# Large loads issued by GpSimd instead of SyncE in a decode attention and feed-forward kernel

## The chip, the cores and the metric

The kernel runs on one core of a Trainium2 chip. A core has five engines that each work through a queue of their own: TensorE (PE, matrix products), VectorE (DVE), ScalarE (ACT), GpSimd (POOL) and SyncE (SP, which only issues transfers and waits). Sixteen DMA engines carry data between memory (HBM) and the core's on-chip buffer. The metric is device microseconds (us) from launch to end; the median of a few executions is given.

## The reference, cut to what matters

One decoding step for four sequences: attention over a cache of 4096 positions with 32 heads, a gated feed-forward block beside it, and a sigmoid gate that mixes the two. Everything is float32.

```
x: (4, 1, 512)   k_cache, v_cache: (4, 32, 4096, 128)
g = sigmoid((x * gate_w).sum(-1))
q = x @ wq                                   # 512 x 4096
p = softmax((q . k_cache) * 128 ** -0.5)     # per sequence and head
a = (p . v_cache) @ wo                       # wo 4096 x 512
b = (gelu(x @ w_gate) * (x @ w_up)) @ w_down # 512 x 1792, 512 x 1792, 1792 x 512
out = g * a + (1 - g) * b
```

The keys and values are 268 MB each, the weights together 28 MB. Each byte is read once.

## The kernel before, in words

The caches are cut into 32 blocks (`NT`), numbered `i`; block `i` holds four heads of one sequence. A block of keys or of values is one load of 128 partitions x 16384 float32, 64 KB for each partition, 8.389 MB in all. Everything large lives in one buffer, `big`, in which zones are handed on by offset: `wq` lies where the values will lie (`VA`), the gate weight `w_gate` follows `wq` in the same place, key blocks alternate between two zones that overlap by a quarter, and values have one zone.

For each block VectorE does the work on the keys in two parts, because the two key zones share a quarter: first the shared quarter (`products(i, True)`, line 384, then `sums(i, True)`, line 390), after which the next key block may land, then the other three quarters (`products(i, False)`, `sums(i, False)`), then three short steps of `soft_max`. ScalarE makes the weights `PM` (line 402). TensorE multiplies them with the values in `pv(i - 1)` (line 416), after which the next value block may land.

`Plan` records every step in program order with the bytes that it reads and writes, and works out for each what it has to wait for. Steps of PE, DVE and ACT are played in loops; steps of the other engines are written out one by one. A step's `lane` names the semaphore that it counts up: a load has one that belongs to its zone or tensor, whichever engine issues it.

All large loads go through one helper, `load` (line 258): `wq`, the key and value blocks, the feed-forward weights, and `wo` in eight pieces at the end. The rest are two small loads that ScalarE issues (`x` and `gate_w`) and two stores of the result that SyncE issues (line 616).

The opening, that is the load of `wq`, the two small loads and the load of key block 0, is played inside a critical section of the tile framework; then the framework's context is closed, and all that follows is played without it:

```
with tc.tile_critical(sync_engine=mybir.EngineType.Pool, no_gpsimd_drain=True):
    plan.play(plan.steps[:opening])
tc.close()
```

`tc.close()` puts a barrier of all five engines into the program, twice, in which GpSimd is the engine that gathers the others' arrivals and releases them. Each engine's part of it begins with a drain, an instruction that lets the engine's earlier work end first. Only behind it stand the steps that prepare `x` (GpSimd's identity matrix `ident`, TensorE's transposes at line 312, VectorE's copies `xT` at line 317), the projection of the queries (line 330), the folding of the query onto its heads (lines 347 to 374), and the loads of `w_gate` and `w_up`, which wait until TensorE has used `wq`.

Of the kernel before, what the change touches and what calls it, by code (L numbers as in the profile page):

```python
# [19 lines left out]
class Plan:  # L20
# [18 lines left out]
    def add(self, engine, emit, reads=(), writes=(), lane=None, unit=1):  # L39
        lane = lane or engine  # L40
        self.units[lane] = unit
        row = self.by_lane.setdefault(lane, [])
        step = Step(lane, engine, emit, self.turn if engine in self.loops else None)
        step.at = len(row)
        need = {}
        for accesses, writing in ((reads, False), (writes, True)):
            for name, lo, hi in accesses:
                for other, a, b, wrote in self.past.get(name, ()):
                    if a < hi and lo < b and (wrote or writing):
                        if other.lane == engine and engine == "pe":  # L50
                            continue
                        if other.lane == engine and not wrote:
                            continue
                        need[other.lane] = max(need.get(other.lane, -1), other.at)
        seen = self.seen[engine]
        for l, n in sorted(need.items(), key=lambda x: -len(self.by_lane[x[0]])):
            if seen.get(l, -1) >= n:
                continue
            other = self.by_lane[l][n]
            other.asked = True  # L60
            step.waits[l] = n
            seen[l] = n
            for k, v in self.knew[other].items():
                seen[k] = max(seen.get(k, -1), v)
        step.waits = {l: n for l, n in step.waits.items()
                      if not any(self.knew[self.by_lane[m][k]].get(l, -1) >= n for m, k in step.waits.items() if m != l)}
        self.knew[step] = dict(seen)
        self.knew[step][lane] = step.at
        if row and lane == engine:
            for k, v in self.knew[row[-1]].items():  # L70
                if k != lane:
                    self.knew[step][k] = max(self.knew[step].get(k, -1), v)
        for accesses, writing in ((reads, False), (writes, True)):
            for name, lo, hi in accesses:
                old = self.past.get(name, [])
                if writing:
                    old = [x for x in old if not (lo <= x[1] and x[2] <= hi)]
                self.past[name] = old + [(step, lo, hi, writing)]
        row.append(step)
        self.steps.append(step)  # L80
        return step
# [51 lines left out]
def tile_gated_mix(tc: tile.TileContext, x, kc, vc, wq, wo, w_gate, w_up, w_down, gate_w, out):  # L133
    nc = tc.nc
# [108 lines left out]
    add = plan.add  # L243
    V, A, T, G = nc.vector, nc.scalar, nc.tensor, nc.gpsimd
# [11 lines left out]
        return g if plan.k is None else plan.k  # L256

    def load(dst, src, writes, lane):
        return add("sp", lambda: nc.sync.dma_start(dst, src), (), writes, lane=lane, unit=16)

    def load_kv(kind, i):
        src = (vc, kc)[kind == "k"]
        a = KB_ * (i % 2) if kind == "k" else VA if i < NT - 1 else 0
        s = src[i % B, HT * (i // B):HT * (i // B) + HT].rearrange("h (p r) d -> (h p) (r d)", p=PH)
        load(place(a, TW), s, [z(a, TW)], "vl" if kind == "v" and i == NT - 1 else kind)
# [7 lines left out]
    def load_f(s):  # L273
        load(place((F0, F1)[s], KC * F), (w_gate, w_up)[s].rearrange("(p c) n -> p (c n)", c=KC),
             [z((F0, F1)[s], KC * F)], f"f{s}")

    def load_d():
        load(place(D0, FC * DM), w_down.rearrange("(p i) n -> p (i n)", i=FC), [z(D0, FC * DM)], "k")
# [326 lines left out]
    for h in range(2):  # L605
# [4 lines left out]
        for c, move in ((2 * h + 1, act), (2 * h, dve)):  # L610
            dst, read, write = res[:B, slice(*COLS[c])], [(("acc", "po0")[h], 0, C4)], [("res", *COLS[c])]
# [46 lines left out]
```

## Time and profile before

| | |
|---|---|
| median of 3 runs | 1309.09 us (1309.06 to 1309.27) |
| span of the profiled execution, first to last instruction | 1307.7 us |
| around it, to the median | 1.4 us |
| HBM read | 564.67 MB, 432 GB/s over the span |
| busy: PE, DVE, ACT, POOL | 354.1, 1158.2, 87.3, 0.7 us |

The time of the profiled execution itself is given as its span alone; what launch and end add is taken as the 1.4 us between it and the median. Busy times are sums over a span in which several engines work side by side. In the rows of the trace "SPq" is an instruction with which SyncE issues a transfer (it ends long before the transfer does), and "<-" behind a row names what ended the idle time ahead of it. "Landing" is the point at which all 16 DMA engines have reported the end of a transfer.

### The profile page before, as it was taken

How to read it: one execution, taken by the hardware profiler on the slowest of the kernel's cores; microseconds unless marked ns; L12 is line 12 of the kernel's file. 1: busy time of each engine (PE TensorE's matmuls, PEld its weight loads, DVE VectorE, ACT ScalarE, POOL GpSimd, SP SyncE). 2: the span in 40 equal slices, each digit the busy share in tenths (PEclk: the TensorE clock that was granted, in tenths of full speed). 3: DMA queues.
4: the chain of work that ended last, by engine and by line, in shares of the span. 5: the costliest groups of instructions: out<-in, count | busy, mean ns of one | idle time of the engine just before them, and what ended most of it. 6: DMA issues, size and time to landing. Idle time of an engine off the chain costs nothing.

```text
span 1307.7 us, 6169 instructions
## 1 busy us (share of the span) xinstructions
PE 354.1 (27%) x2512; PEld 100.8 (8%) x2512; DVE 1158.2 (89%) x303; ACT 87.3 (7%) x291; POOL 0.7 (0%) x6
## 2 busy tenths in 40 slices
PE   3402233201332211322221223321133322122227
PEld 0100001000010000100000000100001000000002
DVE  1899999999899998989989888998989898898992
ACT  0000000000000000000000000000000000000001
POOL 0000000000000000000000000000000000000000
PEclk9656666556666556666656666665666665576669
DMA  9999999999999999999999999999999999999998
GB/s 417 417 446 427 440 439 425 443 425 443 427 441 425 441 425 441 431 437 439 427 443 425 443 427 441 425 441 425 441 431 437 439 427 443 425 443 427 439 428 370
DMA packets 10986, 564.83 MB, mean 432 GB/s; under 512 B 1232, under 2 KB 1752, under 8 KB 1888
## 3 DMA queue, kind: packets, MB, share of 16 engines
q1 hardware_dynamic: 10960, 564.67, 99.7%
q8 instruction: 7, 0.11, 0.0%
q10 hardware_dynamic: 16, 0.02, 0.0%
q14 instruction: 3, 0.02, 0.0%
HBM read 564.67 MB, written 0.01 MB: 432 GB/s over the span
## 4 chain that ended last, share of the span: by engine, by line
DMA 71%; DVE 28%; issue 1%; PE 0%; ACT 0%; SPq 0%; DVEq 0%; POOLq 0%
DMA big<-in_A_k_cache 69%; DVE big L384 14%; DVE sc L390 13%; DMA big<-in_A_wo 2%; PE acc L505 0%; PE wide L497 0%; PE po L505 0%; DVE hT L537 0%; DVE big L535 0%; DVE big L534 0%; DVE big L532 0%; ACT big L511 0%; DVE m L395 0%; ACT big L533 0%; DVE big L530 0%
## 5 line engine op out<-in xcount | busy, mean ns | idle before, releaser
L384 DVE TENSOR_TENSOR big<-big,qb 128x4096 f32<-128x4096 f32 x64 | 556.0, 8687 | 88.8 <-DMA big<-in_A_k_cache 88.8
L390 DVE TENSOR_REDUCE sc<-big 128x32 f32<-128x4096 f32 x64 | 555.9, 8686 | 2.3
L416 PE MATMUL po<-big,PM 128*32 128x512 f32 x2048 | 293.4, 737 | 903.1 <-DMA big<-in_A_v_cache 903.1
L416 PEld LDWEIGHTS po<-big,PM 128*32 128x32 f32 x2048 | 72.3, 132 | 1117.8 <-DMA big<-in_A_v_cache 825.2
L402 ACT ACTIVATE PM<-sc,nb 32x128 f32<-32x128 f32 x128 | 67.2, 525 | 476.5 <-DVE nb L397 429.0
L424 ACT ACTIVATE o<-po 128x512 f32<-128x512 f32 x16 | 9.6, 597 | 443.9 <-PE po L416 443.9
L402 ACT ACTIVATION_READ_ACCUMULATOR PM<-sc,nb 32x1 f32 x128 | 26.1, 204 | 0.0
L374 ACT ACTIVATE qb<-q 128x512 f32<-128x512 f32 x8 | 4.8, 597 | 249.6 <-PE q L372 249.6
L347 DVE TENSOR_TENSOR big<-po,amask 128x512 f32<-128x512 f32 x2 | 1.3, 686 | 19.3 <-PE po L330 19.3
L433 PE MATMUL sm<-o,sel 128*16 128x128 f32 x128 | 15.4, 273 | 5.8 <-ACT o L424 5.8
L330 PE MATMUL po<-big,xT 128*32 128x512 f32 x64 | 10.0, 793 | 18.6 <-DMA big<-in_A_wq 18.6
L518 PE MATMUL q<-big,xT 128*32 128x448 f32 x64 | 10.8, 848 | 13.7 <-DMA big<-in_B_w_gate 11.0
L433 PEld LDWEIGHTS sm<-o,sel 128*16 128x16 f32 x128 | 11.7, 97 | 14.4 <-ACT o L424 13.1
L615 DVE COPY res<-acc 4x144 f32<-4x144 f32 x1 | 0.3, 296 | 13.2 <-PE acc L505 13.2
L372 PE MATMUL q<-QM,hc 128*128 128x512 f32 x16 | 9.9, 706 | 4.2 <-DVE hc L368 4.2
L395 DVE TENSOR_REDUCE m<-sc 128x1 f32<-128x128 f32 x32 | 9.2, 286 | 1.1
L440 DVE RECIPROCAL ri<-sm 16x1 f32<-16x1 f32 x8 | 1.2, 156 | 8.2 <-PE sm L435 8.2
L396 DVE STREAM_TRANSPOSE mt<-m 128x32 f32<-128x32 f32 x32 | 6.8, 212 | 1.1
L397 DVE TENSOR_REDUCE nb<-mt 128x1 f32<-128x32 f32 x32 | 6.0, 186 | 1.1
L497 PE MATMUL wide<-big 128*32 128x512 f32 x46 | 5.6, 596 | 2.3 <-DMA big<-in_A_wo 2.3
L518 PEld LDWEIGHTS q<-big,xT 128*32 128x32 f32 x64 | 3.3, 159 | 20.5 <-issue 20.5
L330 PEld LDWEIGHTS po<-big,xT 128*32 128x32 f32 x64 | 2.7, 139 | 25.1 <-issue 25.1
(74 smaller groups left out, 58.3 us busy)
## 6 DMA issues: line engine op xcount, KB each, us to landing
big<-in_A_wo SPq DMA_DIRECT2D x1, 4096.0 KB, 28.7
big<-in_B_w_gate SPq DMA_DIRECT2D x1, 3584.0 KB, 17.6
big<-in_B_w_up SPq DMA_DIRECT2D x1, 3584.0 KB, 25.8
big<-in_B_w_down SPq DMA_DIRECT2D x1, 3584.0 KB, 19.4
big<-in_A_wo SPq DMA_DIRECT2D x1, 1792.0 KB, 26.3
big<-in_A_wo SPq DMA_DIRECT2D x1, 1280.0 KB, 29.0
big<-in_A_k_cache SPq DMA_DIRECT2D x32, 29.7
big<-in_A_v_cache SPq DMA_DIRECT2D x32, 29.4
```

What stands on the lines that cost most here:

```text
L330: last = T.matmul(PO[s][32 * j:32 * j + 32].rearrange("p j d -> p (j d)"), xTf[:, c, :32], w[:, n0:n0 + HB * D], start=c == 0, stop=c == K ...
L372: pe(lambda: T.matmul(q.rearrange("p b d -> p (b d)"), HC.rearrange("p h k -> p (h k)"), QM.rearrange("p b d -> p (b d)"), start=True, sto ...
L384: dve(lambda: V.tensor_tensor(k, k, QB[:, b:b + 1, :].to_broadcast([P, r1 - r0, D]), op=OP.mult), m + t("qb"), m)
L390: dve(lambda: V.tensor_reduce(SC[i % 2][:, r0:r1], k, axis=AX.X, op=OP.add), [z(KA(i) + r0 * D, (r1 - r0) * D)], [(f"sc{i % 2}", r0, r1)])
L395: dve(lambda: V.tensor_reduce(M1[n], SC[n], axis=AX.X, op=OP.max), t(f"sc{n}"), t(f"m1{n}"))
L396: dve(lambda: V.transpose(MT, M1[n].to_broadcast([P, PH])), t(f"m1{n}"), t("mt"))
L397: dve(lambda: V.tensor_reduce(NB[n], MT, axis=AX.X, op=OP.max, negate=True), t("mt"), t(f"nb{n}"))
L402: last = A.activation(PM[:, PZ:].rearrange("p (c m) -> p c m", m=32)[s, :, h:RJ * HT:HT], SC[n][s, :].rearrange("p (c j) -> p c j", j=RJ), ...
L416: last = T.matmul(PO[n][32 * c:32 * c + 32].rearrange("p j d -> p (j d)"), PM[:, m0:m0 + 32], place(VAT(i) + j * N, N), start=b == 0 and j ...
L424: act(lambda: A.activation(O[n], PO[n], AF.Copy), t(f"po{n}"), t(f"o{n}"))
L433: T.matmul(sm[:B * HT, :D], selv[:, j, m0:m0 + B * HT], O[n][:, j, :], start=(n, j) == (0, 0), stop=(n, j) == (N - 1, RJ - 1))
L518: last = T.matmul(q.rearrange("p b d -> p (b d)")[32 * j:32 * j + 32, :FG], xTf[:, c, :32], place((F0, F1)[s] + c * F + j * FG, FG), start ...
```

## The change: who issues the loads

The helper `load` records its step for GpSimd instead of SyncE, and issues it there. Every load that goes through it moves; the waits worked out for it and the semaphore that it counts up stay. A transfer that SyncE issues uses a hardware queue, one that GpSimd issues a software queue.

```
     def load(dst, src, writes, lane):
-        return add("sp", lambda: nc.sync.dma_start(dst, src), (), writes, lane=lane, unit=16)
+        return add("pool", lambda: G.dma_start(dst, src), (), writes, lane=lane, unit=16)
```

The rows of the built program on GpSimd around the opening; "barrier ... gather" is the barrier of `tc.close()`, `Pool_sequencer_49`, `Pool_49` and `Activation_sequencer_49` belong to the critical section, L298 and L299 make `ident`. Drains are not listed among the rows: one stands on GpSimd directly ahead of each of the two barriers, before and now. Before:

```order
L622 NO_OP
L625 UNCONDITIONAL_BRANCH
L622 NO_OP [waits SP_sequencer_49,Activation_sequencer_49,Pool_sequencer_49]
L625 UNCONDITIONAL_BRANCH
L625 ISA [waits barrier_Pool_Activation_PE_DVE_SP_gather]
L298 MEMSET ident 128x128 [waits barrier_Pool_Activation_PE_DVE_SP_gather]
L299 ISA [waits lane_pool]
L299 AFFINE_SELECT ident<-ident 128x128
```

and now:

```order
L625 UNCONDITIONAL_BRANCH [waits Pool_sequencer_49]
L259 DMA big<-in_A_wq 128x16384
L259 DMA big<-in_A_k_cache 128x16384
L622 UNCONDITIONAL_BRANCH
L622 NO_OP [waits Pool_49]
L622 NO_OP [waits Activation_sequencer_49,Pool_sequencer_49]
L625 UNCONDITIONAL_BRANCH
L625 ISA [waits barrier_Pool_Activation_PE_DVE_SP_gather]
L298 MEMSET ident 128x128 [waits barrier_Pool_Activation_PE_DVE_SP_gather]
L299 ISA [waits lane_pool]
L299 AFFINE_SELECT ident<-ident 128x128
L259 DMA big<-in_B_w_gate 128x7168 [waits lane_pe]
```

The two opening loads now stand in GpSimd's queue ahead of the barrier and of `ident`; before, they stood in SyncE's queue, and GpSimd had nothing of its own between the critical section and the barrier. All later loads follow on GpSimd behind `ident`, in the order that they had on SyncE.

At the end of the program SyncE had the last loads and then the stores:

```order
L259 DMA big<-in_A_v_cache 128x16384 [waits lane_dve]
L259 DMA big<-in_B_w_down 128x7168 [waits lane_pe]
L259 DMA big<-in_A_wo 128x8192
L259 DMA big<-in_A_wo 128x3584 [waits lane_dve]
L616 DMA out_0<-res 4x288 [waits lane_fin0]
L616 DMA out_0<-res 4x224 [waits lane_fin1]
L635 ISA [waits lane_out]
```

and now its whole program is:

```order
L654 UNCONDITIONAL_BRANCH [waits barrier_Pool_Activation_PE_DVE_SP_release]
L625 UNCONDITIONAL_BRANCH x2
L616 DMA out_0<-res 4x288 [waits Activation_sequencer_49,Pool_sequencer_49,Pool_49,barrier_Pool_Activation_PE_DVE_SP_release,lane_fin0]
L616 DMA out_0<-res 4x224 [waits lane_fin1]
L635 ISA [waits lane_out]
```

The rows of PE, DVE and ACT are the same in both programs.

## The prediction

> **What bounds the kernel now.** I began with the page: the engines' busy times, the slices with the DMA engines' share, the queues, and the chain of work that ended last.
>
> ```profile
> span 1307.7 us, 6169 instructions
> PE 354.1 (27%) x2512; PEld 100.8 (8%) x2512; DVE 1158.2 (89%) x303; ACT 87.3 (7%) x291; POOL 0.7 (0%) x6
> DMA  9999999999999999999999999999999999999998
> q1 hardware_dynamic: 10960, 564.67, 99.7%
> DMA 71%; DVE 28%; issue 1%; PE 0%; ACT 0%; SPq 0%; DVEq 0%; POOLq 0%
> big<-in_A_wq SPq DMA_DIRECT2D x1, 21.8
> ```
>
> The DMA engines have no idle slice, and SyncE's queue (q1) fills 99.7% of them. The chain names DMA and VectorE, because a key block's landing lets VectorE work and VectorE's work lets the next key block go. Which of the two sets the pace is seen in the windows (the last two columns are the DMA engines' busy share and GB/s) and in one turn of the timeline.
>
> ```profile
> 166.00:1200.00 1034.00, 270.02 (x1868) 74.24 (x1868) 949.76 (x207) 68.88 (x236) 0.00 (x0) 0.63 1.00 434
> 1302.00:1302.90 0.90, 0.20 (x7) 0.10 (x8) 0.00 (x0) 0.60 (x1) 0.00 (x0) 1.00 0.93 358
> ```
>
> ```profile
> 127.59 0.33 SPq L259 DMA_DIRECT2D big<-in_A_k_cache  x1
> 137.77 8.87 PE L416 MATMUL po<-big,PM 128*32 128x512 f32 x64 [29.20 <-DMA big<-in_A_v_cache]
> 146.71 0.33 SPq L259 DMA_DIRECT2D big<-in_A_v_cache  x1
> 157.06 4.43 DVE L384 TENSOR_TENSOR big<-big,qb 128x4096 f32<-128x4096 f32 x1 [2.85 <-DMA big<-in_A_k_cache]
> ...
> 165.85 12.95 DVE L384 TENSOR_TENSOR big<-big,qb 128x12288 f32<-128x12288 f32 x1
> 165.97 0.33 SPq L259 DMA_DIRECT2D big<-in_A_k_cache  x1
> 178.83 12.95 DVE L390 TENSOR_REDUCE sc<-big 128x96 f32<-128x12288 f32 x1
> ...
> 195.68 4.42 DVE L384 TENSOR_TENSOR big<-big,qb 128x4096 f32<-128x4096 f32 x1 [3.11 <-DMA big<-in_A_k_cache]
> ...
> 1209.28 0.33 SPq L259 DMA_DIRECT2D big<-in_A_k_cache  x1
> ```
>
> From the key issue at 127.59 to that at 1209.28 lie 28 turns, so a turn is 38.63 us. It moves two blocks of 8.389 MB: 434 GB/s, the rate of the window, in which the DMA engines are 1.00 busy; a block takes 19.33 us. VectorE idles 2.85 to 3.11 us of a turn. So the transfers bound the loop. The queue always holds work: the key load is issued at 127.59, 10.2 us before the values ahead of it are used at 137.77; the value load at 146.71, 10.35 us before the keys ahead of it at 157.06. The time is therefore the start of the first transfer, plus 564.67 MB at 434 GB/s (1301 us), plus whatever makes the DMA engines idle. What decides this change is whether it opens a gap.
>
> **The loop, after the change.** Each of the 62 or so loads in the turns is issued by GpSimd, on the same waits. SyncE's issue takes 0.33 us; GpSimd's is nowhere in this trace. It may be a little quicker, or take as long as the slowest issue of the program, 2.46 us:
>
> ```profile
> L259 SPq DMA_DIRECT2D big<-in_A_wo x8: 328/432/2463, 1267.1 to 1276.5; - x8
> ```
>
> Either lies within the 10 us for which the queue has work, so I cost it at nothing. If that cover were gone, each load would cost its full extra, up to 2.1 us x 64 = 136 us. GpSimd has 0.7 us of other work, so nothing queues behind a load that waits, except the next load, as on SyncE. The `wo` pieces at the end are issued from 1267 on and used from 1295.86 on, so eight slower issues are also hidden. SyncE's stores lose the queue that stood ahead of them, but they wait for the result: nothing.
>
> **The opening is the place that moves.** These rows are the timeline from launch to the third key load.
>
> ```profile
> 0.89 0.40 SPq L259 DMA_DIRECT2D big<-in_A_wq  x1
> 1.35 0.42 SPq L259 DMA_DIRECT2D big<-in_A_k_cache  x1
> 2.87 0.20 POOL L298 MEMSET ident<- 128x128 f32 x1 [2.43 <-POOLq L625]
> 5.39 0.89 DVE L317 COPY xT<-sg 128x128 f32<-128x128 f32 x4
> 22.88 9.99 PE L330 MATMUL po<-big,xT 128*32 128x512 f32 x64 [18.58 <-DMA big<-in_A_wq]
> 32.93 0.33 SPq L259 DMA_DIRECT2D big<-in_B_w_gate  x1
> 39.16 0.60 ACT L374 ACTIVATE qb<-q 128x512 f32<-128x512 f32 x1 [35.00 <-PE q L372]
> 42.15 4.43 DVE L384 TENSOR_TENSOR big<-big,qb 128x4096 f32<-128x4096 f32 x1 [5.16 <-DMA big<-in_A_k_cache]
> 50.66 5.89 PE L518 MATMUL q<-big,xT 128*32 128x448 f32 x32 [11.02 <-DMA big<-in_B_w_gate]
> 51.06 0.33 SPq L259 DMA_DIRECT2D big<-in_A_k_cache  x1
> 59.19 1.45 PE L518 MATMUL q<-big,xT 128*32 128x448 f32 x8 [2.64 <-DMA big<-in_B_w_up]
> 69.48 0.33 SPq L259 DMA_DIRECT2D big<-in_A_v_cache  x1
> 92.16 0.33 SPq L259 DMA_DIRECT2D big<-in_A_k_cache  x1
> 99.17 9.39 PE L416 MATMUL po<-big,PM 128*32 128x512 f32 x64 [35.07 <-DMA big<-in_A_v_cache]
> ```
>
> Today SyncE issues `wq` and key block 0 by 1.77, all engines pass the barrier of `tc.close()` by 2.87, and the preparation of `x` and the projection run under those two transfers. In the new order both loads stand on GpSimd ahead of its drain and of the barrier that releases every engine. The question is when that drain ends. Lower bound: when the loads are issued; SyncE's drain does that, since it issued at 1.35 and everything ran at 2.87, 39 us before the block landed. Upper bound: when both have landed, at 42.15. SyncE's row is the nearest, but it is a hardware queue's. I take the landing: a load that GpSimd issues is GpSimd's own work rather than one handed to another unit, and the code of the critical section carries a switch that leaves out GpSimd's drain and no other engine's, which would be pointless if it were short. `tc.close()` has no such switch here. No row of before settles it; both ends stay, as likeliest case and as rival.
>
> The Trainium skill has the rule for a drain under PSUM — Partial Sum Buffer, section Engine vs sequencer instructions: "drain waits for the engine to go fully idle". By it the release comes at the landing, if a load in flight counts as GpSimd's; no run here shows that yet.
>
> The sum, with the landing:
> 1. First transfer: later by one more issue of SyncE's length, 0.40 us (row 0.89), bounds -0.3 and +2.1. The block lands at 42.55.
> 2. Barrier: from SyncE's last issue (1.77) to `ident` (2.87) 1.1 us; release at 43.65.
> 3. From release to the end of `xT`: 6.28 - 2.87 = 3.41; at 47.06. (VectorE's gate steps no longer wait and fit beside the projection.)
> 4. Projection, 22.88 to 32.93: 10.05; `w_gate` is issued at 57.11 instead of 32.93. `w_gate` overwrites `wq`, so it can't go sooner.
> 5. The DMA engines have been idle since 42.55. A load into an idle queue pays a start: `wq` took 21.8 us from issue to landing against 19.33 at 434 GB/s, so 2.47 us. `w_gate` (3.67 MB, 8.46 us) lands at 57.11 + 8.46 + 2.47 = 68.04 instead of 50.66: **17.4 us later**.
> 6. VectorE's first product: from the issue of `w_gate` to the query spread is 39.76 - 32.93 = 6.83, so 63.94 instead of 42.15: 21.8 later. It is now later than the transfers by 4.4, so the queue's lead shrinks. Key block 1 is issued at 72.9, with the DMA busy until 76.6 (lead 3.7); values 0 at 91.3 against 95.9 (4.6); key block 2 at 114.0 against 116.6 (2.6, the tightest). All are over the start of 2.47, barely. From then on VectorE, with 3 us to spare in a turn, gains back the 4.4 in two turns, and the loop stays bound by transfers.
> 7. The end is unchanged, only later.
>
> Sum: 1309.1 + 17.4 = **1326.5 us**. I add to the profiled execution's 1307.7 the same 1.4 around it as the median shows. The likeliest case's own range: if a start costs only SyncE's issue, 0.4, it is 1324; if the tight leads of step 6 each cost up to the 2.1 of a slow issue, and the first one too, 1309.1 + 17.4 + 4 x 2.1 = 1335.
>
> **Rivals.**
> - The drain does not wait for landing. For it: SyncE's row. Then only step 1 is left, since everything from 2.87 to 22.88 has 18.58 us of idle cover on TensorE: 1309.5 us, range 1308.8 to 1311.2. Not slower; it is decided by whether `ident` starts near 4 or near 44 us.
> - A lower rate through the software queue, on top. For it: small packets cost rate here (358 GB/s at 1302, where `wo` pieces of about 1 KB per partition move). Against: nothing in the change alters the blocks' 64 KB rows. If all moved at 358 the transfers would take 1577 us, 276 more, so 1603; a loss of 1% is 13 us, 1340.
> - VectorE holds up GpSimd's loads. The key load is issued 0.12 us after a 12.95 us product starts (165.85, 165.97). Were it held until 178.8, the queue would run dry at 176 and each key block land 178.8 + 21.8 = 200.6 instead of 195.68, 4.9 us a turn, x 30 = 147 more: 1474. It decides only beyond the 10.2 us lead. No row speaks for it.
> - Slightly faster, 1306 or below: the blocks would have to move 0.2% above 434 GB/s with the drain harmless. Nothing speaks for it.
>
> The skill warns of the third under SBUF — State Buffer, section Who interferes with whom: VectorE copies and scalar operations in a two-port mode lock GpSimd out of descriptor writing, two-input products and reductions do not. By that rule only short steps could hold a load, such as the one below, 0.23 us against a lead of 10 us, and the loop stays as forecast; no run shows it yet.
>
> ```profile
> L368 DVE TENSOR_SCALAR hc<-hmask 128x128 f32 x7 | 1.6, 227 | 1.1 <-issue 1.0
> ```
>
> **How the numbers follow.** The drain case alone 0.82, no drain 0.09, a lower rate (with the drain) 0.05, held loads 0.02, faster 0.02. 0.2% is 2.6 us, about what a measurement of this kernel can tell from no change. Slower: 0.82 + 0.05 + 0.02 = 0.89; within 0.2%: 0.09; faster: 0.02. The range 1319 to 1336 takes in the drain case's 1324 to 1335, some room below for a barrier that lets engines go earlier, and a rate loss up to 0.7%; it leaves out 0.2, mostly the case without the drain.
>
> **What the new profile would show.** Right: GpSimd's `ident` and the other engines' first rows near 44 us; TensorE's projection at about 47 to 57; a hole of some 15 us in the GB/s slices at about 43 to 58; then 434 GB/s and the same 38.63 us turn, shifted by about 17. VectorE's idle ahead of line 384 gone in the first two or three turns. Wrong: `ident` near 4 us (then no change), a turn longer than 38.7 us (rate, or held loads, told apart by whether the DMA share stays 1.00), or gaps ahead of key loads in the first turns (step 6).

## The result, and the profile after

The changed kernel takes 1327.91 us (median of 4 runs, 1327.38 to 1328.55) against 1309.07 us before in the same session: a ratio of 1.0144, 95% interval 1.013 to 1.0159. That is 18.8 us more; 17.4 were forecast. The profiled execution has a span of 1326.1 us, 18.4 more than before.

The page of the changed kernel: its span, the DMA engines' share and rate in 40 slices, and the queue of the loads.

```profile
span 1326.1 us, 6169 instructions
DMA  9499999999999999999999999999999999999998
GB/s 410 202 434 439 437 421 439 434 437 431 435 437 425 441 435 439 425 437 435 437 431 435 437 425 441 435 437 427 437 435 435 433 435 437 425 443 431 437 427 367
q0 software_dynamic: 10560, 564.66, 98.4%
```

Nearly all of the loss lies in one slice, the second: its rate is 202 GB/s where every slice of before is at 417 or more but the last. (The first slice, 410 against 417, has the later start of the transfers.) Behind it the slices read as before, though each load now runs in the software queue q0. The windows confirm it (the last two columns are the DMA share and GB/s):

```profile
43.00:58.00 15.00, 9.56 (x68) 2.75 (x68) 6.96 (x25) 1.28 (x1) 1.56 (x4) 1.00 0.02 4
186.00:1218.00 1032.00, 267.59 (x1868) 73.81 (x1868) 947.31 (x208) 68.87 (x236) 27.96 (x53) 0.63 1.00 434
```

A hole of 15 us in the transfers, then 434 GB/s, the rate of before. The timeline of the changed kernel's opening shows what made the hole:

```profile
1.50 0.67 POOL L259 DMA_DIRECT2D big<-in_A_wq  x1 [1.05 <-PEq L625]
2.16 0.53 POOL L259 DMA_DIRECT2D big<-in_A_k_cache  x1
44.01 0.20 POOL L298 MEMSET ident<- 128x128 f32 x1 [41.32 <-POOLq L625]
46.52 0.88 DVE L317 COPY xT<-sg 128x128 f32<-128x128 f32 x4
47.46 8.92 PE L330 MATMUL po<-big,xT 128*32 128x512 f32 x64 [2.03 <-DVE xT L317]
56.73 0.55 POOL L259 DMA_DIRECT2D big<-in_B_w_gate  x1 [11.99 <-PE po L330]
62.45 4.42 DVE L384 TENSOR_TENSOR big<-big,qb 128x4096 f32<-128x4096 f32 x1 [1.94 <-ACT qb L374]
68.18 4.94 PE L518 MATMUL q<-big,xT 128*32 128x448 f32 x32 [5.88 <-DMA big<-in_B_w_gate]
...
112.73 0.53 POOL L259 DMA_DIRECT2D big<-in_A_k_cache  x1 [22.15 <-DVE sc L390]
116.58 8.50 PE L416 MATMUL po<-big,PM 128*32 128x512 f32 x64 [33.61 <-DMA big<-in_A_v_cache]
```

`ident`, the first work behind the barrier, starts at 44.01 us; it started at 2.87. GpSimd had issued both loads by 2.69 and then did nothing for 41.32 us. The longest time from issue to landing of the changed kernel's loads is that of key block 0:

```profile
DMA to landing us min/median/max: 11.3/29.4/41.0
```

2.16 + 41.0 = 43.16, and 0.85 us later `ident` starts. The drains themselves stand in the view of line 625: how often each engine ran one there, the shortest, middle and longest in ns, and when the first and the last began. GpSimd's and SyncE's before, then GpSimd's of the changed kernel:

```profile
L625 POOLq DRAIN  x3: 34/41/60, 2.2 to 2.6; - x3
L625 SPq DRAIN  x3: 7/7/7, 2.2 to 2.5; - x3
```

```profile
L625 POOLq DRAIN  x3: 40/78/41103, 2.2 to 43.7; - x3
```

Before, SyncE's drains took 7 ns with both its loads in flight. Now the first of GpSimd's drains begins at 2.2 and lasts 41.1 us, so it ends at 43.3, with the landing. The waits of the critical section, which also stand between the loads and `ident`, are over when it begins, so they aren't what takes the time. The projection then runs with nothing in flight, and `w_gate` waits for it. In the loop GpSimd's issue is 0.53 us long, and key loads 27 turns apart are (1227.22 - 183.82) / 27 = 38.64 us apart, the turn of before:

```profile
183.82 0.53 POOL L259 DMA_DIRECT2D big<-in_A_k_cache  x1 [18.09 <-DVE sc L390]
...
1227.22 0.53 POOL L259 DMA_DIRECT2D big<-in_A_k_cache  x1 [19.23 <-DVE sc L390]
```

### The profile page after: what moved, and what is told of

Same layout as the page of the kernel before. It is cut to its first block, busy times and chain, and to the rows that moved or that the text cites. A ratio compares the mean times of both kernels' runs of the same rounds, so it can differ in the third digit from the quotient of the medians.

```text
span 1326.1 us, 6169 instructions
## 1 busy us (share of the span) xinstructions
PE 350.2 (26%) x2512; PEld 99.6 (8%) x2512; DVE 1158.2 (87%) x303; ACT 87.4 (7%) x291; POOL 40.9 (3%) x82
## 4 chain that ended last, share of the span: by engine, by line
DMA 66%; DVE 28%; issue 1%; PE 1%; ACT 0%; POOL 0%; DVEq 0%; POOLq 0%
DMA big<-in_A_k_cache 64%; DVE big L384 14%; DVE sc L390 13%; DMA big<-in_A_wo 2%; PE po L330 1%; PE acc L505 0%; PE wide L497 0%; DVE big L350 0%; DVE big L347 0%; PE po L505 0%; PE q L372 0%; DVE hT L537 0%; DVE PM L307 0%; DVE xT L317 0%; DVE big L535 0%
## 5 line engine op out<-in xcount | busy, mean ns | idle before, releaser
L259 POOL DMA_DIRECT2D big<-in_A_v_cache x32 | 16.9, 528 | 599.8 <-PE po L416 563.9
L259 POOL DMA_DIRECT2D big<-in_A_k_cache x32 | 16.9, 528 | 575.5 <-DVE sc L390 575.5
```

Source lines behind the costliest of these rows:

```text
L259: return add("pool", lambda: G.dma_start(dst, src), (), writes, lane=lane, unit=16)
```

## The experiments

Two theories stood against each other. D: GpSimd's drain ahead of the barrier lasts until GpSimd's loads have landed, so everything behind the barrier starts late. Q: the software queue itself costs the time, and the barrier only happens to stand there. The first four kernels ran on one chip, with 1309.21 us for before.

**The opening alone given back to SyncE (e1).** The edit, in `load` (recorded before `opening` is set for the first two loads; they get a semaphore of their own):

```
+        if opening is None:
+            return add("sp", lambda: nc.sync.dma_start(dst, src), (), writes, lane=lane + "0", unit=16)
         return add("pool", lambda: G.dma_start(dst, src), (), writes, lane=lane, unit=16)
```

> Only the loads of wq and key block 0 go back to SyncE; the other 74 stay on GpSimd. Theory D (GpSimd's drain ahead of the barrier of tc.close() waits until GpSimd's loads have landed): ident starts near 2.9 us as before, no gap at 43 to 58 us, time 1309.1 within 0.8 us. Rival Q (the software queue itself is the cost: a slow first start, or something lost with each load, and the barrier only happens to stand there): w_gate becomes the first software load, a gap of 5 us or more opens near it or the turns lengthen beyond 38.64 us, and the time stays above 1314 us.

Measured: 1310.39 us, ratio 1.0009 (1.0 to 1.0018). `ident` starts at 2.88 and no hole is left, so 17.6 of the 18.8 us are gone with two of 76 loads. Q falls. D's account of the hole holds, but the time is 0.5 us above what D allowed, and the interval begins at 1.0: the remaining 1.2 us are at the edge of what these runs can tell from nothing. The timeline of this kernel shows something new:

```profile
32.26 0.67 POOL L263 DMA_DIRECT2D big<-in_B_w_gate  x1 [28.66 <-PE po L334]
45.58 4.43 DVE L388 TENSOR_TENSOR big<-big,qb 128x4096 f32<-128x4096 f32 x1 [9.54 <-DMA big<-in_A_k_cache]
95.85 0.53 POOL L263 DMA_DIRECT2D big<-in_A_k_cache  x1 [22.15 <-DVE sc L394]
99.09 8.35 PE L420 MATMUL po<-big,PM 128*32 128x512 f32 x64 [36.52 <-DMA big<-in_A_v_cache]
```

Key block 0, in SyncE's queue, is used 3.4 us later than before (42.15), though it was issued at the same time: once `w_gate` is issued in GpSimd's queue at 32.26, the DMA engines divide themselves between the two. VectorE is late by as much, and key block 2 is issued 3.2 us ahead of the end of the values instead of 7.0.

**The opening alone on GpSimd**, the other 74 loads on SyncE (the same edit with the two branches exchanged).

> Only the loads of wq and key block 0 are GpSimd's; the other 74 go back to SyncE. D: ident near 44 us, gap of about 15 us from 43 to 58 us, time 1326.5 to 1328, nearly all of the 18.8 us. Q: with two software loads in place of 76, less than a third of the 18.8 us is left, 1309 to 1315.

Measured: 1327.75 us, ratio 1.0139 (1.0123 to 1.0154), `ident` at 43.76. Two software loads cost as much as 76. This is D's value; Q gave at most 1315. The sums are not quite the same: the first values are used at 116.52, as late as in the changed kernel (116.58; before, 99.17), but key block 2, issued only 2.4 us ahead of that, lands 20.8 us behind it; in the changed kernel it lands 19.3 us behind.

**All loads on GpSimd, the opening's behind the barrier:**

```
-        plan.play(plan.steps[:opening])
+        plan.play([s for s in plan.steps[:opening] if s.engine == "act"])
     tc.close()
     tc.compile()
...
+    plan.play([s for s in plan.steps[:opening] if s.engine != "act"])
     plan.play(plan.steps[opening:first])
```

> All 76 loads on GpSimd, but the two of the opening are issued behind the barrier of tc.close() instead of ahead of it; ScalarE's two small loads stay ahead. D: nothing is in flight from GpSimd at the drain, so the barrier passes at about 2.9 us and wq is issued at about 3.0 us instead of 0.89; 2.1 us for that and 0.3 to 0.9 us for the slower software issue: 1311.9 (1311 to 1313.5). Q: as the changed kernel or worse, 1327 to 1330.

Measured: 1312.08 us, ratio 1.0022 (1.0013 to 1.0031), 2.87 us above before. Its first windows, then those of before, show the start of the transfers:

```profile
0.00:4.70 4.70, 0.00 (x0) 0.00 (x0) 0.27 (x2) 1.28 (x1) 1.51 (x7) 1.00 0.01 3
4.80:5.80 1.00, 0.42 (x4) 0.42 (x4) 0.36 (x4) 0.00 (x0) 0.29 (x2) 1.00 2.30 786
```

```profile
0.00:1.90 1.90, 0.00 (x0) 0.00 (x0) 0.00 (x0) 0.00 (x0) 0.20 (x4) 1.00 0.02 2
1.90:2.90 1.00, 0.00 (x0) 0.00 (x0) 0.00 (x0) 0.03 (x1) 0.03 (x1) 1.00 2.90 987
```

The data begin to flow between 4.7 and 4.8 us instead of at 1.9, so 2.8 to 2.9 later: the whole difference, as D had it; Q gave 1327 or more. That leaves nothing measurable for 76 software loads in the loop and the tail.

**A smaller dose: `wq` ahead of the barrier, key block 0 behind it.**

```
-        plan.play(plan.steps[:opening])
+        plan.play(plan.steps[:opening - 1])
...
-    plan.play(plan.steps[opening:first])
+    plan.play(plan.steps[opening - 1:first])
```

> A smaller dose: all loads on GpSimd, wq ahead of the barrier, key block 0 behind it. D: the drain ends when wq has landed, about 1.5 + 22.4 = 23.9 us, ident and the issue of key block 0 at about 24.8 us; key block 0 lands at about 24.8 + 22.4 = 47.2 instead of 42.15; the projection (28.9 to 37.9) and w_gate's issue are covered by it; time 1309.1 + 5.0 = 1314.1 (1312.5 to 1315.5). Q: as the changed kernel, 1327, or with no step between.

Measured: 1314.37 us, ratio 1.004 (1.0024 to 1.0055). The view by queue and the timeline of this kernel:

```profile
big<-in_A_wq POOLq DMA_DIRECT2D x1, 22.4
```

```profile
1.50 0.67 POOL L259 DMA_DIRECT2D big<-in_A_wq  x1 [1.05 <-PEq L625]
25.11 0.54 POOL L259 DMA_DIRECT2D big<-in_A_k_cache  x1 [22.94 <-POOLq L625]
47.27 4.43 DVE L384 TENSOR_TENSOR big<-big,qb 128x4096 f32<-128x4096 f32 x1 [4.82 <-DMA big<-in_A_k_cache]
```

`wq` lands at 1.50 + 22.4 = 23.9, GpSimd goes on 1.2 us later, and block 0 is used at 47.27, 5.1 us later than before. The time grows by 5.2 us, inside D's range and far from the changed kernel's 1327.9.

The next three ran on another chip, with 1309.05 us for before. They were to settle what the first experiment had left over, and to give a dose smaller still.

**The opening and the two feed-forward weights on SyncE** (the first edit, with the two loads of `load_f` added to its condition).

> As e1, but w_gate and w_up also go back to SyncE; 72 loads stay on GpSimd. In e1 the DMA engines shared themselves between SyncE's key block 0 and GpSimd's w_gate, so the block was used at 45.58 instead of 42.15 us, and key block 2 was issued only 3.2 us ahead of the end of the values before it. Theory I (that sharing is what left e1 1.2 us above before): the block at 42.15 again, key block 2 about 6.5 us ahead, time 1309.2 (1308.8 to 1309.6). Rival P (each software load costs a little in the loop): 72 of 74 software loads are left, so still 1310.2 to 1310.6.

Measured: 1316.12 us, ratio 1.0055 (1.0041 to 1.0069): neither theory's value. Block 0 is used at 42.19, as theory I had it, but I overlooked that the edge between the queues had only moved, to `w_up` and key block 1:

```profile
32.49 0.43 SPq L262 DMA_DIRECT2D big<-in_B_w_up  x1
51.38 0.67 POOL L263 DMA_DIRECT2D big<-in_A_k_cache  x1 [47.78 <-DVE sc L394]
70.04 5.60 PE L522 MATMUL q<-big,xT 128*32 128x448 f32 x32 [14.30 <-DMA big<-in_B_w_up]
80.70 0.53 POOL L263 DMA_DIRECT2D big<-in_A_v_cache  x1 [28.65 <-DVE hT L541]
103.36 0.53 POOL L263 DMA_DIRECT2D big<-in_A_k_cache  x1 [22.13 <-DVE sc L394]
103.70 9.70 PE L420 MATMUL po<-big,PM 128*32 128x512 f32 x64 [28.06 <-DMA big<-in_A_v_cache]
```

```profile
50.00:70.00 20.00, 5.04 (x32) 1.42 (x32) 14.77 (x8) 0.54 (x1) 0.67 (x1) 0.59 1.00 432
79.00:82.00 3.00, 0.00 (x0) 0.00 (x0) 2.96 (x3) 0.00 (x0) 0.53 (x1) 0.50 0.41 131
102.20:104.80 2.60, 1.09 (x8) 0.39 (x12) 2.60 (x2) 0.00 (x0) 0.53 (x1) 0.50 0.62 205
```

From 50 to 70 the engines are full (1.00, 432 GB/s) but from 51.38 on serve two queues, so `w_up` is used at 70.04 instead of 59.19. The view by queue of the stretch from 55 to 65 us shows both, with the share of the engines' time that each takes:

```profile
q0 software_dynamic: 48, 3.15, 72.6%
q1 hardware_dynamic: 48, 1.38, 32.2%
```

That holds up the feed-forward step, the value load at 80.70 and the key load at 103.36. The first finds the engines idle and the second comes 0.3 us before they would be, in the two windows with shares of 0.41 and 0.62. The profiled execution took 1317.95 us, 1.8 more than the median.

**The feed-forward weights alone on GpSimd (e7).** The kernel before, with `w_gate` and `w_up` alone issued by GpSimd.

> The other half: only w_gate and w_up are GpSimd's, the other 74 loads are SyncE's. I: key block 0 used at about 45.5 us, key block 2 about 3 us ahead, time 1309.8 to 1310.6. P: two software loads cost nothing, 1309.0 to 1309.4.

Measured: 1309.77 us, ratio 1.0012 (1.0003 to 1.0021); block 0 is used at 45.49, and key block 2 is issued at 95.49, 3.75 us ahead of the values' use at 99.24. Two software loads out of 76 lead to 0.7 of the 1.2 us that e1 had left over, at the low edge of what I allowed; rival P's 1309.4 is passed by 0.4.

The remainder is explained only in part. The late key block 0 is the sharing: at 45.58 and 45.49 us where `w_gate` runs in the other queue, at 42.15 and 42.19 where it doesn't. That it costs time is shown for e1 alone, and not for all of it. Counted from the DMA packets of the traces, the 16 engines idle as follows, on average, around the start of key block 2:

| kernel | key block 2 issued ahead of the values' use | idle there |
|---|---|---|
| changed | 3.85 us | 0.08 us |
| feed-forward weights alone on GpSimd (e7) | 3.75 us | none |
| opening on SyncE (e1) | 3.24 us | 0.43 us |
| opening alone on GpSimd | 2.38 us | 0.45 us |
| opening and feed-forward weights on SyncE | 0.34 us | 2.7 us |

So e1 loses 0.4 us to its short lead, and e7 loses none there or anywhere from 60 to 1290 us. What makes up the rest of e1's 1.2 us and the 0.7 us of e7 stays open. It isn't a price of each software load: the kernel with all 76 on GpSimd behind the barrier has nothing left over beyond its later start.

**The two small loads on GpSimd, everything large on SyncE.** This moves lines 292 and 293 from `nc.scalar` to `nc.gpsimd`.

> The kernel before, but ScalarE's two small loads (x and gate_w, 8 KB each) are issued by GpSimd ahead of the barrier; all large loads stay on SyncE. D: the drain waits for their landing too, which shares the DMA engines with wq: ident at 7 to 12 us instead of 2.9, and, because TensorE waits for wq until 22.9 us anyway, time 1309.2 within 0.6 us. Were the drain to end when the loads are issued, ident would start near 3.5 us, with the same time.

Measured: 1309.33 us, ratio 1.0001 (0.9992 to 1.0011). The view by queue and the timeline:

```profile
big<-in_gate_w POOLq DMA_DIRECT2D x1, 8.0 KB, 13.8
```

```profile
1.36 0.42 SPq L259 DMA_DIRECT2D big<-in_A_k_cache  x1
2.14 0.52 POOL L293 DMA_DIRECT2D big<-in_gate_w  x1
16.77 0.20 POOL L298 MEMSET ident<- 128x128 f32 x1 [14.11 <-POOLq L625]
```

`gate_w` lands at 2.14 + 13.8 = 15.94, later than I had thought, and `ident` follows 0.83 us behind, so a load of 8 KB holds the barrier as one of 8 MB does. SyncE's two large loads are in flight all the while and hold nothing. It costs no time, since TensorE waits for `wq` until 23.3 us in this kernel.

## Why the prediction was right

The likeliest case came in, and four doses show the step on which it rested, the choice of the upper bound for the drain. GpSimd's first work behind the barrier started 0.8 to 1.2 us after its last load landed, wherever that was: at 16.77 (landing 15.94), 25.11 (23.9), 43.76 (2.16 + 40.8 = 42.96, the opening alone) and 44.01 us (43.16). Its longest drain in each of the other three doses, in the same order:

```profile
L625 POOLq DRAIN  x3: 40/86/13860, 2.2 to 16.5; - x3
L625 POOLq DRAIN  x3: 40/67/21817, 2.2 to 24.4; - x3
L629 POOLq DRAIN  x3: 34/78/40854, 2.2 to 43.5; - x3
```

Begun at 2.2, they end at 16.1, 24.0 and 43.1, each within 0.2 us of the landing. SyncE's row, which I had named as the nearest and taken as the lower bound, does not carry over from a hardware queue. The rule that I quoted from the Trainium skill (PSUM — Partial Sum Buffer, section Engine vs sequencer instructions), that a drain waits for the engine to be fully idle, agrees with these four doses, in which a load that GpSimd issued counts as its work until it lands. A load of SyncE doesn't count as SyncE's: its drains took 7 ns with both loads in flight.

By its steps:
- First transfer: taken at 0.4 us. GpSimd's first issue starts 0.61 us after SyncE's did and is 0.67 us long against 0.40; both are in the rows, and block 0 lands at 43.16 instead of the forecast 42.55. This term was 0.6 us too small, inside its bounds.
- Barrier, 1.1: 0.85. From release to the end of `xT`, 3.41: 47.40 - 44.01 = 3.39. Projection, 10.05: about 9.3, from 47.46 to the issue of `w_gate` at 56.73. The sum of these, issue of `w_gate` at 57.11, came out 0.38 too late.
- The restart of an idle queue, 2.47 on top of 8.46: `w_gate` is used at 68.18 after its issue at 56.73, 11.45 us; 10.93 were forecast. Use at 68.18 against 68.04. That the sum agrees to 0.14 us is luck: errors of +0.6, -0.25, -0.7 and +0.5 us offset each other.
- The leads: key block 2, forecast to be the tightest with 2.6 us, had 116.58 - 112.73 = 3.85. VectorE's first product waits for the query spread and starts at 62.45 (forecast 63.94), because the spread took 5.70 us from the issue of `w_gate` where 6.83 were taken. The step's condition was too weak, and here the outcome was lucky: it asked for a lead above 2.47 us, but a lead of 3.24 left the engines idle for 0.43 us in e1. The 2.6 us that were forecast would probably have cost about half a microsecond.
- The loop at no cost: the turn is 38.64 us, the rate 434 GB/s, and the longer issue (0.53 against 0.33 us) vanishes in the lead of 10 us.

The last 1 us of span (18.4 against 17.4) comes in behind `w_gate`. The first values are used 17.41 us later than before (116.58 against 99.17), the last but one 17.69 (1276.00 against 1258.31), and the last 18.38 (1296.22 against 1277.84). Why the last block of values loses 0.7 us stays open, as do the few tenths in the loop.

The rivals: no drain is out by the four doses. A lower rate is out by the windows. A hold-up by VectorE is out: GpSimd's key issue is 0.53 us long while VectorE's 12.95 us product runs, and its value issue, in the rest of the loop, is the same. The clearest case is the key load at 103.36 in the kernel with the opening and the feed-forward weights on SyncE: a 12.95 us product had begun at 102.98, the engines were about to run dry, and the load landed 22.0 us after its issue, as `wq` did in an idle queue (21.8 to 22.4). Held until the product's end at 115.93, it would have taken 12 us more. The Trainium skill (SBUF — State Buffer, section Who interferes with whom) says that reductions never contend with GpSimd on this chip, and infers that two-input products do not stall the writing of descriptors; the landing after 22.0 us and the turn agree.

## What to carry to other kernels

Before moving a load to GpSimd, look for the barriers and drains behind it in GpSimd's queue: a drain there lasts until GpSimd's loads have landed, while one on SyncE passed 39 us before SyncE's load did. The load's own price, 0.53 us of issue instead of 0.33, is nothing where the queue has work ahead of it; a lead of 3.75 us was enough here and 3.24 us was not. When loads that depend on order are split over two queues, look at who shares the DMA engines at the edge between them.

## What the runs showed that I had not expected

Two queues do not serve loads in the order of their issue. With `w_up` in SyncE's queue from 32.49 and key block 1 in GpSimd's from 51.38, the engines stayed at 432 GB/s and yet `w_up` was used 10.9 us later than before, because it had to share with a load issued 19 us after it. At a full rate the sum of bytes does not change, but the first load is finished late, and what hangs on it cost 7 us here. The Trainium skill states that a DMA engine goes round robin between the queue rows that have work (DMA: Bandwidth & Descriptors, section Queues, rings and completion order); these rows agree with it.
